# Eighteen attention blocks with their output transposed by DMA, modulations as column tiles, and a third chunk transposed by DMA, in one transformer block on one core

## The chip, the cores and the metric

The kernel runs on one core of a Trainium2 chip. A core has five engines with an instruction queue each: TensorE (PE in the profile) multiplies matrices, VectorE (DVE) and ScalarE (ACT) work element by element, GpSimd (POOL) does small things here, and SyncE (SP) issues transfers. Sixteen DMA engines move data between HBM and the core's SBUF, and within SBUF; transfers are issued from SyncE's queue (q1 in the profile) or ScalarE's (q10). Each engine works through its own queue in order. Matmul results go to eight PSUM banks, from which VectorE or ScalarE evicts them.

The metric is the device time of one execution, in microseconds: the median of several runs.

## The reference

One transformer block for a sequence of 2048 tokens of 448 features, all in bfloat16. A vector `c` gives six modulation vectors; attention has 16 heads of 28 features, and each token sees itself and 7 earlier tokens, at distances 0, 2, ..., 14.

```python
mod = (_silu(c) @ w_mod).reshape(c.shape[0], 6, 1, -1)
sa, ca, ga, sb, cb, gb = (mod[:, 0].copy(), mod[:, 1].copy(), ..., mod[:, 5].copy())
h = _layernorm(x, axis=-1) * (1 + ca) + sa
x = x + ga * _A_ref(h, A_wqkv, A_wo)
h = _layernorm(x, axis=-1) * (1 + cb) + sb
x = x + gb * _B_ref(h, B_w1, B_b1, B_w2, B_b2)
```

`_A_ref` is the attention with its output projection `wo`; `_B_ref` is a second layernorm, `w1` to 1792 features, gelu, and `w2` back to 448.

## The kernel before

**Token order.** All tokens that attend to each other have the same parity, so the kernel keeps even tokens first (1024) and odd tokens after them. In this order a token sees itself and its 7 predecessors: a band. There are 16 token blocks of 128 (`x_all`, line 313), and four chunks of 512 (`CH`).

**Front end** (`front_end`, line 550). For 2 or 4 token blocks: statistics on VectorE (line 446), the reciprocal root on GpSimd (469, 471), normalisation into `zbuf` (477 or 480), then the transposition that puts features on partitions (`hT`). For chunks 0 and 1 that is four TensorE transposes a block (line 577), whose eviction also applies `sa` and `1 + ca` (586, 589). For chunks 2 and 3 (`Z_DMA = (2, 3)`, line 79) it is a DMA transpose from SyncE's queue (line 569), after which VectorE modulates `hT` in place (589). Chunk 0 is done as two halves of 256 tokens. Then come eight projections for q and k (599), each four matmuls of 256 or 512 columns, evicted at 434 or 436.

**Attention** (`attention`, line 664). 17 blocks of 121 queries (`BQ`), each with a window of 128 keys: logits of 16 heads as four row tiles of TensorE (678), four exponentials on ScalarE (689), a product with a mask of 2048 columns on VectorE (696), V (711) and its eviction, the weighted sums with a column of ones for the denominator (721), the division (728, 732). The block's output `on` is transposed by four TensorE transposes (742) and copied from PSUM to `oT` (434 or 436). `oT` feeds the output projection of a token block (`wo_item`, 763), which is added to x (768). Blocks of 121 queries straddle token blocks and the border between even and odd tokens.

**Second half.** For two token blocks at a time (`norm_items`, 770): layernorm, scale and shift (787), second layernorm into `ybuf`, a DMA transpose on SyncE (803). For a chunk (`mlp_items`, 818): the up-projection (295 and 300), gelu on ScalarE (812), the down-projection (853), the last addition (866, 868) and the store (872).

**Modulations.** `sa` and `ca` are made as columns at the start (511). The other four (`mod_item`, 618) are each made with a matrix whose 128 columns all hold silu(c), so that every partition of the result has the vector (623, 448 columns, four matmuls); `ga` is multiplied into `wo_s` (631), `gb` into `w2_s` (648).

**Order.** The instructions of an engine stand in an order that a planner (`Plan.order`, line 108) makes at build time, from costs, due times of the loads (`LANDS`), priorities (`PRI`, `NUDGE`), buffer slots and PSUM banks. `PHASES` says how many attention blocks stand before each chunk's up-projection. The first loads and memsets (355 to 425) come before everything planned; among them the loads of w1 (283, 284) and w2 (425) are SyncE's last before its first transpose. Eight semaphores are used in turn for all transfers, so a transfer is issued only when the one eight places before it has landed.

Of the kernel before, what the change touches and what calls it, by code (L numbers as in the profile page):

```python
# [9 lines left out]
FP32 = mybir.dt.float32  # L10
# [6 lines left out]
KT = 4  # L17
KOFF_N = [0, 128, 256, 320]
ZR_N = 64
# [3 lines left out]
PADF = 16  # L23
BQ, BK = 121, 128
NBK = -(-S // BQ)
WT = PADF + S + PADF
# [5 lines left out]
PHASES = [9, 14, 17, 17]  # L32
# [4 lines left out]
LANDS = [("c", 3.0), ("x0", 5.1), ("wmsa", 6.2), ("wmca", 6.8), ("x2", 8.3), ("wk", 8.6), ("wq", 10.2), ("later", 10.0),  # L37
         ("wv", 11.4), ("x4", 12.4), ("wmod2", 17.4), ("wo", 19.1), ("b2", 19.1), ("x8", 22.0), ("w1", 28.7),
         ("w2", 31.0)]

NIDLE = [8, 3, 3, 4]
PLANS = None

LOOK = 0.000444

PRI = {"ad": -96.0, "agfst": 196.2, "ags2": 257.8, "ags3": 51.1, "ex": -118.3, "ge": -9.0, "h": 492.2,
       "lt": 26.7, "mk": -63.3, "ml": 15.5, "mod": -71.9, "on": -63.1, "ot": -130.2, "pb": -18.2, "po": 77.9,
       "ps": 105.4, "pt": 35.7, "pv": 19.9, "qe": -91.5, "qk": -123.7, "r3": 22.0, "rd": -24.1, "s2": -207.6,
       "s3": 72.9, "ve": -158.2, "w1": -18.3, "w2": -62.8, "wo": -144.0, "wt": 10.8, "x1": 20.5, "y": -37.1,
       "yt": -87.3, "z": 139.3, "z2": 81.0, "zt": -267.4}  # L50

NUDGE = {"ad10": -20.7, "ad6": -81.4, "ad8": 11.5, "ags2_0": 10.6, "ags2_11": -6.6, "ags2_14": -75.9,
       "ags2_2": -100.4, "ags2_5": -6.3, "ags2_8": -10.9, "ags3_11": -15.8, "ags3_14": 104.5, "ags3_3": 36.6,
       "ags3_5": -16.0, "ags3_7": -64.8, "ex11.2": 12.3, "fin9": -40.2, "frs12a": 19.8, "frs8a": 22.6,
       "ge2.10": 13.7, "ge2.8": 76.9, "ge3.12": 31.1, "h12.0": 37.1, "h4.2": 55.2, "h8.2": 78.5, "lt0": 93.2,
       "lt10": 29.5, "lt12": 5.8, "lt13": 52.0, "lt15": -33.2, "lt2": -20.6, "lt4": 58.9, "lt8": -8.9,
       "mk5": 34.4, "mk8": 47.0, "ml10": -42.6, "ml4": 10.8, "on12": -18.4, "on4": 8.5, "ot11": 74.0,
       "ot12": 9.8, "ot16": 53.8, "ot4": 60.9, "ot5": 22.7, "ot6": 65.9, "out13": -24.4, "out14": -59.4,
       "out8": -106.6, "pb_cbe": -184.9, "pb_gb": -36.7, "pb_gbe": -13.6, "po0": 8.9, "po1": -60.3, "po12": 10.8,
       "po15": -157.0, "pt10": 41.4, "pt12": 14.3, "pt5": -52.4, "pt8": -37.2, "pv1": -38.0, "pv13": -62.4,  # L60
       "pv4": 11.4, "pv7": 25.6, "qe12.0": -27.8, "qe12.3": 18.7, "qe12.5": 61.8, "qe2.0": -34.0, "qe2.1": 132.4,
       "qe2.2": 4.0, "qe2.3": 19.6, "qe2.4": 7.9, "qe2.6": 9.4, "qe2.7": -33.6, "qe4.0": 62.7, "qe4.7": -12.7,
       "qe8.0": 5.1, "qe8.1": -64.2, "qe8.7": -80.1, "qk0.1": 133.8, "qk12.0": 113.6, "qk12.6": 61.1,
       "qk4.1": -47.9, "qk4.3": 67.4, "qk4.4": 55.2, "qk4.5": -100.0, "qk4.7": 76.7, "qk8.7": -37.3,
       "r2_0": -89.0, "r2_0a": 57.1, "r2_10": 15.5, "r2_4": -9.3, "r2_6": -40.7, "r2_8": -62.2, "r3_0": 23.2,
       "r3_0a": 24.8, "r3_10a": -7.1, "r3_12": -88.9, "r3_12a": -80.6, "r3_6": 21.3, "r3_6a": -73.9, "r3_8": 9.0,
       "r3_8a": 38.0, "rd12": 24.6, "rd13": 26.1, "rd4": 14.1, "rd6": 54.8, "s2_11": 64.8, "s2_15": -82.0,
       "s2_5": -15.7, "s2_6": 35.8, "s2_8": 10.9, "s3_0": -51.5, "s3_1": 12.8, "s3_10": 26.8, "s3_11": 17.0,
       "s3_12": 28.7, "s3_13": -42.2, "s3_7": 38.2, "s3_9": -24.9, "w1_0.5": 32.1, "w1_1.6": 54.9, "w1_2.0": 6.1,
       "w1_2.2": -19.8, "w1_3.6": 57.3, "w2_11.1": 53.2, "w2_14.2": 103.0, "w2_14.3": 80.6, "w2_14.6": -16.7,  # L70
       "w2_15.2": -35.7, "w2_4.3": -44.4, "w2_5.6": 48.3, "w2_8.2": 135.9, "w2_9.2": 147.8, "w2_9.3": -21.2,
       "w2_9.4": -70.7, "w2_9.5": 107.8, "w2s2": 74.7, "wo0": 8.8, "wo1": 19.3, "wo11": -16.1, "wo8": 34.2,
       "wt_0.5": -16.3, "wt_2.3": -8.1, "wt_2.5": 20.1, "x1_1": 21.7, "x1_10": -25.3, "x1_11": -5.0,
       "x1_5": 27.9, "y11": -18.1, "y5": 40.1, "yt1": 28.5, "yt10": -133.2, "yt11": -10.4, "yt12": -68.4,
       "yt2": 6.1, "z1": 95.3, "z2": 138.5, "z2_10": 23.2, "z2_11": -10.3, "z2_12": -125.8, "z2_13": 16.8,
       "z2_2": 8.2, "z2_4": 21.3, "z2_5": 19.0, "z2_8": 41.6, "z2_9": 13.3, "z4": 6.2, "z8": 12.9, "zt13": -4.0,
       "zt4": 5.5, "zt8": 84.8}
STATS_ACT = 2.0
Z_DMA = (2, 3)
# [160 lines left out]
def kernel(  # L240
# [68 lines left out]
    hT = cst.tile([128, KT, WT], BF16, name="hT")  # L309
    qT = cst.tile([128, 4, WT], BF16, name="qT")  # L310
    kT = cst.tile([128, 4, WT], BF16, name="kT")
# [5 lines left out]
    silu_bc = cst.tile([128, KT, 128], BF16, name="silu_bc")  # L317
# [9 lines left out]
    g2_bc = cst.tile([128, D], BF16, name="g2_bc")  # L327
    sb_bc = cst.tile([128, D], BF16, name="sb_bc")
    gb_bc = cst.tile([128, D], BF16, name="gb_bc")
    gbb2_bc = cst.tile([128, D], FP32, name="gbb2_bc")  # L330
    ident = cst.tile([128, 128], BF16, name="ident")
    mask1 = cst.tile([128, BK], BF16, name="mask1")
    mask_rest = cst.tile([128, H, BK], BF16, name="mask_rest")
# [4 lines left out]
    ybufs = [cst.tile([128, DP], BF16, name=f"ybuf{i}") for i in range(NYB)]  # L338
    NVB = 3
    vbufs = [cst.tile([128, H, DH + 1], BF16, name=f"vbuf{i}") for i in range(NVB)]  # L340

    wmod2 = cst.tile([128, KT, 4 * D], BF16, name="wmod2")
# [3 lines left out]
    silu_bf = cst.tile([128, KT], BF16, name="silu_bf")  # L346
# [9 lines left out]
    wmod = stp.tile([128, KT, 2, DP], BF16, name="wmod")  # L356
    wqk_st = stp.tile([128, KT, 2 * D], BF16, name="wqk_st")
    nc.scalar.dma_start(out=x_all[:, 0:2, :], in_=xv[:, 0, 0:2, :])
    load_ktiles(nc.sync, wmod[:, :, 0, 0:D], w_mod[:, 0:D], 0)
    load_ktiles(nc.scalar, wmod[:, :, 1, 0:D], w_mod[:, D:2 * D], 0)  # L360
    nc.scalar.dma_start(out=x_all[:, 2:4, :], in_=xv[:, 0, 2:4, :])
    load_ktiles(nc.sync, wqk_st[:, :, D:2 * D], A_wqkv[:, D:2 * D], 0)
    load_ktiles(nc.sync, wqk_st[:, :, 0:D], A_wqkv[:, 0:D], 0)
    load_ktiles(nc.sync, Wv, A_wqkv[:, 2 * D:3 * D], 0)
    nc.sync.dma_start(out=x_all[:, 4:8, :], in_=xv[:, 0, 4:8, :])
    load_ktiles(nc.sync, wmod2, w_mod[:, 2 * D:6 * D], 0)
    load_ktiles(nc.sync, wo_s, A_wo, ZR_N)
# [9 lines left out]
    def idle(n, out):  # L377
        for i in range(n):
            nc.tensor.matmul(out, lhsT=idle_in[:, 0:128], rhs=idle_in[:], start=True, stop=True)

    idle(4, psum[7][:])
    c_col = stp.tile([128, KT], FP32, name="c_col")
    nc.vector.memset(c_col[:], 0.0)
    nc.vector.memset(wmod[64:128, KT - 1, :, :], 0.0)
    nc.vector.memset(wmod[:, :, :, D:DP], 0.0)
    nc.vector.memset(Wqk[64:128, KT - 1, :, :], 0.0)
    for zb in zbufs:
        nc.vector.memset(zb[:, D:DP], 0.0)
    nc.vector.memset(Wv[64:128, KT - 1, :], 0.0)
# [21 lines left out]
    def tok_col(b):  # L411
        return PADF + b * 128

# [521 lines left out]
```

## Time and profile before

| what | value |
|---|---|
| time, median of 3 runs | 182.32 us (181.95 to 182.45) |
| the profiled execution | 182.19 us, span 180.5 us |
| granted TensorE clock | 1.00 |
| busy PE / DVE / ACT / POOL | 174.4 / 138.4 / 118.6 / 32.7 us |
| matmuls | 1464 |
| DMA | 14.63 MB, HBM read 9.41 MB |
| q1 (SyncE's queue) | 22334 packets, 13.53 MB |
| q10 (ScalarE's queue) | 1024 packets, 0.86 MB |

The span is the time from the first to the last instruction; the rest of an execution's time lies around it. The profile lists, for each line, engine and shape, how often an instruction ran, how long one took on the mean, and what its engine had waited for. Matmuls overlap, so the mean of one (0.35 us for 448 columns) is its latency and not its price. The chain of waits follows the work back from the last instruction, at each step to what released it; its pieces add up to the span.

### The profile page before, as it was taken

Reading aid. Unit: us, or ns where it says so; the run is one execution under the profiler, and the core shown is the slowest. Engines: PE = TensorE matmul, PEld = TensorE weight load, DVE = VectorE, ACT = ScalarE, POOL = GpSimd, SP = SyncE. Lnnn points to the kernel's source line nnn. Section 1 sums busy time; section 2 is a strip of 40 time slices with the busy share of each in tenths; the row PEclk is TensorE's granted clock in tenths of the full one; section 3 lists DMA queues with packets and bytes.
Section 4 is the critical chain, followed back from the end, with each engine's and each line's share of the span. In section 5 each row is a group of like instructions: output and inputs, shape, how many; then the busy total and the mean of one; then the engine's idle time right before and its main releaser. Section 6 shows DMA issues by size and latency. Waiting matters only on the chain.

```text
span 180.5 us, 3837 instructions
## 1 busy us (share of the span) xinstructions
PE 174.4 (97%) x1464; PEld 88.4 (49%) x1464; DVE 138.4 (77%) x348; ACT 118.6 (66%) x217; POOL 32.7 (18%) x67
## 2 busy tenths in 40 slices
PE   6989999999999999999999999999999999999992
PEld 2457566555555544444655454445643454433451
DVE  5789899799998999997989988688879865020251
ACT  2298996999898946999578475995835810077400
POOL 8413005000106403121403041100013400000000
PEclk9999999999999999999999999999999999999999
DMA  5999995441000530011051012031000025100011
GB/s 166 322 368 315 401 390 162 94 86 29 0 4 0 61 61 0 0 35 32 22 79 35 4 21 63 0 73 41 0 4 25 0 56 120 47 25 0 0 51 51
DMA packets 23376, 14.63 MB, mean 81 GB/s; under 512 B 13693, under 2 KB 22398, under 8 KB 23358
## 3 DMA queue, kind: packets, MB, share of 16 engines
q1 hardware_dynamic: 22334, 13.53, 27.0%
q10 hardware_dynamic: 1024, 0.86, 1.5%
q8 instruction: 11, 0.18, 0.4%
q14 instruction: 7, 0.06, 0.1%
HBM read 9.41 MB, written 1.84 MB: 62 GB/s over the span
## 4 chain that ended last, share of the span: by engine, by line
PE 72%; DVE 12%; DMA 4%; ACT 4%; SPq 2%; issue 2%; ACTq 1%; POOL 1%; DVEq 0%
PE ps L295 21%; PE ps L853 20%; PE ps L599 8%; PE ps L763 6%; PE ps L711 5%; PE ps L300 4%; DVE st L446 4%; DMA hT<-zbuf 3%; PE ps L721 3%; PE ps L678 2%; DVE et L696 2%; PE ps L742 2%; SPq L803 2%; DVE hT L589 2%; DMA yT<-ybuf 1%
## 5 line engine op out<-in xcount | busy, mean ns | idle before, releaser
L812 ACT ACTIVATE hm<-ps,b_col 128x512 bf16<-128x512 f32 x56 | 34.1, 692 | 23.2 <-PE ps L300 23.1
L853 PE MATMUL ps<-w_s,hm 128*128 128x448 bf16 x224 | 47.2, 353 | 0.0
L469 POOL TENSOR_TENSOR rs<-tv,neg_half 128x2 f32<-128x2 f32 (+1 forms) x21 | 20.4, 973 | 108.8 <-DVE ng L465 108.7
L295 PE MATMUL ps<-yT,w_s 128*128 128x512 bf16 x168 | 39.5, 380 | 0.5 <-DMA yT<-ybuf 0.5
L689 ACT ACTIVATE et<-ps 128x512 bf16<-128x512 f32 x68 | 36.1, 613 | 3.3 <-PE ps L678 3.0
L599 PE MATMUL ps<-hT,Wqk 128*128 128x512 bf16 (+1 forms) x160 | 31.3, 337 | 0.9 <-ACT Wqk L436 0.9
L853 PEld LDWEIGHTS <-hm 128*128 128x128 bf16 x224 | 21.0, 98 | 19.3 <-issue 0.9
L295 PEld LDWEIGHTS <-w_s 128*128 128x128 bf16 x168 | 15.5, 98 | 21.9 <-issue 5.3
L866 DVE TENSOR_TENSOR xt<-ps,gbb_bc 128x448 f32<-128x448 f32 x11 | 6.9, 624 | 22.3 <-PE ps L853 22.3
L696 DVE TENSOR_TENSOR et<-et,mask_rest 128x2048 bf16<-128x2048 bf16 x17 | 20.5, 1208 | 0.1
L599 PEld LDWEIGHTS <-Wqk 128*128 128x128 bf16 x160 | 14.6, 97 | 11.4 <-POOL nb L471 1.1
L446 DVE BATCH_NORM_STATS2 st<-x_all 128x6 f32<-128x448 bf16 x32 | 18.5, 613 | 0.1
L711 PE MATMUL ps<-Wv,hT 128*128 128x448 bf16 x68 | 15.7, 353 | 0.0
L763 PE MATMUL ps<-wo_s,oT 128*128 128x448 bf16 x64 | 14.1, 352 | 0.0
L768 DVE TENSOR_TENSOR x_all<-ps,x_all 128x448 bf16<-128x448 f32 x16 | 9.7, 619 | 3.1 <-PE ps L763 3.0
L436 ACT CAST vbuf<-ps 128x448 bf16<-128x448 f32 x14 | 7.6, 546 | 5.0 <-PE ps L711 5.0
L436 ACT CAST qT<-ps 128x512 bf16<-128x512 f32 (+1 forms) x19 | 9.6, 518 | 2.0 <-PE ps L599 1.5
L721 PEld LDWEIGHTS <-et 128*128 128x128 bf16 x272 | 9.0, 96 | 3.8 <-DVE et L696 0.9
L732 DVE TENSOR_TENSOR on<-ps,rden 128x448 bf16<-128x448 f32 x17 | 10.5, 616 | 0.2
L436 ACT CAST kT<-ps 128x512 bf16<-128x512 f32 (+1 forms) x18 | 8.9, 512 | 1.3 <-PE ps L599 1.1
L721 PE MATMUL ps<-vbuf,et 128*128 128x29 bf16 x272 | 9.5, 176 | 0.1
L446 DVE BATCH_NORM_STATS2 st<-z 128x6 f32<-128x448 bf16 x16 | 9.4, 612 | 0.1
(98 smaller groups left out, 188.7 us busy)
## 6 DMA issues: line engine op xcount, KB each, us to landing
w_s<-in_B_w_dram SPq DMA_DIRECT2D x2, 896.0 KB, 11.4
out_dram<-x_all SPq DMA_DIRECT2D x16, 112.0 KB, 1.7
w_s<-in_B_w_dram SPq DMA_DIRECT2D x1, 1568.0 KB, 13.7
wmod<-in_w_mod_dram SPq DMA_DIRECT2D x1, 1344.0 KB, 7.5
x_all<-in_A_x_dram SPq DMA_DIRECT2D x1, 896.0 KB, 10.4
wqk_st<-in_A_wqkv_dram SPq DMA_DIRECT2D x2, 336.0 KB, 5.8
x_all<-in_A_x_dram ACTq DMA_DIRECT2D x2, 224.0 KB, 4.2
x_all<-in_A_x_dram SPq DMA_DIRECT2D x1, 448.0 KB, 5.0
```

The costliest lines, as they stand in the source:

```text
L295: nc.tensor.matmul(o, lhsT=lhs(w, slice(0, 128), kt), rhs=rhs(slice(0, 128), kt), start=(i == 0), stop=False)
L436: nc.scalar.copy(out=out, in_=in_)
L446: nc.vector.bn_stats(out=st[:], in_=src())
L469: nc.gpsimd.tensor_tensor(out=rs[:], in0=T["tv", tile_key][:], in1=neg_half[:, 0:n], op=ALU.pow)
L599: nc.tensor.matmul(pq, lhsT=Wqk[:, kt, m, :], rhs=hT[:, kt, c0:c0 + w], start=(kt == 0), stop=(kt == KT - 1))
L689: nc.scalar.activation(out=et_v[:, r], in_=T["lt", g][r].rearrange("p (ft c) -> p ft c", ft=4), func=ACT.Exp, scale=float(DH) ** -0.5)
L696: nc.vector.tensor_tensor(out=et[:], in0=et[:], in1=mask_rest[:], op=ALU.mult)
L711: nc.tensor.matmul(pv, lhsT=hT[:, kt, k0:k0 + BK], rhs=Wv[:, kt, :], start=(kt == 0), stop=(kt == KT - 1))
L721: nc.tensor.matmul(po[:, h, :], lhsT=T["et", g][:, h, :], rhs=vbufs[g % NVB][:, h, :], start=True, stop=True)
L763: nc.tensor.matmul(pw, lhsT=oT[:, kt, jb * 128:(jb + 1) * 128], rhs=wo_s[:, kt, :], start=(kt == 0), stop=(kt == KT - 1))
L812: nc.scalar.activation(out=T["hm", c][:, ft, 0:w], in_=ps_of(f"p1_{c}.{ft}", w), func=ACT.Gelu_apprx_tanh, bias=b1_col[:, ft:ft + 1])
L853: nc.tensor.matmul(T["p2", b], lhsT=T["hm", c][:, ft, bi * 128:(bi + 1) * 128], rhs=w2_s[:, ft, :], start=(ft == 0 and b not in XPE), stop ...
```

## The change

**Attention blocks.** 18 blocks, nine for each parity: one of 128 queries at the start, then eight of 112. No block crosses the border between parities. The window is 128 keys and ends with the block's last query. Two masks of 128 columns are broadcast over the heads in the product; `mask_rest` and the two memsets on `et` go. `et` and `on` are fixed buffers.

```diff
-BQ, BK = 121, 128
-NBK = -(-S // BQ)
+BLOCKS = [(p * SL + t, n) for p in range(2) for t, n in [(0, BK)] + [(BK + 112 * i, 112) for i in range(8)]]
...
-PHASES = [9, 14, 17, 17]
+PHASES = [9, 16, 18, 18]
...
-Z_DMA = (2, 3)
+Z_DMA = (1, 2, 3)
```

**Output transposed by DMA.** The four TensorE transposes and the copy from PSUM become one DMA transpose on SyncE's queue, from `on` (padded to 512 columns) to `oT`.

```diff
-        def p_fn(e):
-            pt = T["pt", g] = ps_of(f"pt{g}", KT * 64).bitcast(BF16).rearrange("p (kt n) -> p kt n", kt=KT)
-            for kt in range(KT):
-                nc.tensor.transpose(out=pt[:, kt, :], in_=T["on", g][:, KOFF_N[kt]:KOFF_N[kt] + 128],
-                                    identity=ident[:])
...
+        P.add(f"ot{g}", {"SP": 1.25}, needs=[f"on{g}"] + old, uses=[f"on{g}"], lag=1.2,
+              fn=lambda e: nc.sync.dma_start_transpose(out=oT[:, :, c0:c0 + nq], in_=on_of[g][0:nq, :]))
```

**Modulations.** The matrix of silu(c) has 32 columns, and the four vectors are made in one PSUM bank, each in a column tile of 32 (16 matmuls, four column tiles). One eviction adds 1 to `cb`; four rows go to DRAM and come back spread over 128 partitions, both transfers issued from ScalarE's queue. Weights of the modulations are kept as four tiles of 112 rows.

```diff
+    def pb_fn(e):
+        pb = T["pb"] = ps_of("pb", D)
+        for kt in range(KT):
+            for v in range(4):
+                nc.tensor.matmul(pb[32 * v:32 * v + 32, :], lhsT=silu_bc[:, kt, :], rhs=wmod2[:, kt, v * D:(v + 1) * D],
+                                 start=(kt == 0), stop=(kt == KT - 1), tile_position=(0, 32 * v))
...
+    P.add("modw", {"ACT": 0.45}, needs=["pb_e"], lag=2.0,
+          fn=lambda e: nc.scalar.dma_start(out=mod_dram[:], in_=mod_rows[0:128:32, :]))
+    P.add("modr", {"ACT": 0.45}, needs=["modw"], lag=3.0,
+          fn=lambda e: nc.scalar.dma_start(out=mod_bc[:], in_=mod_dram[:].partition_broadcast(128)))
+    P.add("pb_gae", {"DVE": 1.05}, needs=["modr", "wo"], fn=lambda e: nc.vector.tensor_tensor(
+        out=wo_s[:], in0=wo_s[:], in1=mod_bc[:, 0, :].unsqueeze(1).to_broadcast([128, KT, D]), op=ALU.mult))
```

`gb`, `sb` and `1 + cb` are read from `mod_bc` too, where they were copied out of PSUM before.

**Chunk 1.** With `Z_DMA = (1, 2, 3)` the front end of chunk 1 uses DMA transposes as chunks 2 and 3 do. In the order of SyncE's instructions its four transposes stand right after the load of w2, then come two of the attention output, then chunk 2's.

**First loads.** x blocks 0 and 1 come separately on ScalarE's queue, both first modulation matrices in one load, wq and wk in one (three quarters and a rest), and x blocks 2 and 3 on SyncE behind them.

```diff
-    nc.scalar.dma_start(out=x_all[:, 0:2, :], in_=xv[:, 0, 0:2, :])
-    load_ktiles(nc.sync, wmod[:, :, 0, 0:D], w_mod[:, 0:D], 0)
-    load_ktiles(nc.scalar, wmod[:, :, 1, 0:D], w_mod[:, D:2 * D], 0)
-    nc.scalar.dma_start(out=x_all[:, 2:4, :], in_=xv[:, 0, 2:4, :])
-    load_ktiles(nc.sync, wqk_st[:, :, D:2 * D], A_wqkv[:, D:2 * D], 0)
-    load_ktiles(nc.sync, wqk_st[:, :, 0:D], A_wqkv[:, 0:D], 0)
+    for b in range(2):
+        nc.scalar.dma_start(out=x_all[:, b, :], in_=xv[:, 0, b, :])
+    nc.sync.dma_start(out=wmod[:, :, 0:2 * D], in_=w_mod[:, 0:2 * D].rearrange("(kt p) n -> p kt n", p=KM))
+    load_ktiles(nc.sync, wqk_st, A_wqkv[:, 0:2 * D], 0)
+    nc.sync.dma_start(out=x_all[:, 2:4, :], in_=xv[:, 0, 2:4, :])
```

The placement of wq and wk into `Wqk` is done in eight pieces, which may also go to GpSimd. The first transposes use four PSUM banks instead of two. One of the groups of idle matmuls that fill TensorE's first microseconds goes, the others change in size. `LANDS`, `PRI`, `NUDGE` and `LOOK` have new values, so the planner's order is a new one on every engine.

## The prediction

> **What bounds the kernel now.** I read the page's slices first, then busy time by stage, then the chain of waits, then the DMA issues, and the SyncE queue last. The slices (40 of 4.5 us) show TensorE at nine tenths nearly throughout, VectorE close behind until two thirds of the span, and the DMA engines full in slices 2 to 6.
>
> ```profile
> PE   6989999999999999999999999999999999999992
> DVE  5789899799998999997989988688879865020251
> DMA  5999995441000530011051012031000025100011
> ```
>
> By stage (busy us of each engine, granted clock, DMA share, GB/s), both engines are full before 45.6 us, and TensorE alone after it.
>
> ```profile
> 17.00:45.60 28.60, 28.52 (x313) 16.19 (x307) 26.52 (x65) 25.53 (x52) 2.72 (x5) 1.00 0.63 195
> 45.60:66.50 20.90, 20.83 (x214) 11.13 (x214) 20.00 (x53) 18.05 (x35) 5.96 (x8) 1.00 0.18 27
> ```
>
> Busy matmuls overlap, so I take prices from the chain of waits (start, us, what), where each piece is what the next one really had to wait for. From 45.75 on it is an almost unbroken row of matmuls, up to the last addition and store. A group of four transposes of an attention output (L742) costs 0.22 us, a 512-wide projection (L599) 0.86, sixteen weighted sums (L721) 0.40, sixteen logits (L678) 0.34, V (L711) 0.76, one modulation vector (L623) 0.76.
>
> ```profile
> 47.19 0.22 PE ps L742 x4
> ...
> 50.35 0.86 PE ps L599 x4
> 51.22 0.40 PE ps L721 x16
> ...
> 52.48 0.34 PE ps L678 x16
> ...
> 54.65 0.76 PE ps L711 x4
> ...
> 65.72 0.76 PE ps L623 x4
> ...
> 177.33 0.62 DVE x_all L868
> ```
>
> So every microsecond of matmuls taken away is worth up to a microsecond, and every microsecond in which TensorE is left without work costs one.
>
> **What speaks against the change** is in the DMA issues (KB each, us to landing) and in SyncE's own row (start, us).
>
> ```profile
> w_s<-in_B_w_dram SPq DMA_DIRECT2D x1, 1568.0 KB, 13.7
> out_dram<-x_all SPq DMA_DIRECT2D x16, 112.0 KB, 1.7
> x_all<-in_A_x_dram SPq DMA_DIRECT2D x1, 896.0 KB, 10.4
> b_bc<-in_B_b_dram SPq DMA_DIRECT2D x1, 112.0 KB, 9.1
> hT<-zbuf SPq DMA_TRANSPOSE x8, 2.5
> ```
>
> ```profile
> 11.49 0.38 SPq L370 DMA_DIRECT2D x_all<-in_A_x_dram  x1
> ...
> 16.71 0.37 SPq L425 DMA_DIRECT2D w_s<-in_B_w_dram  x1
> 29.42 11.18 SPq L569 DMA_TRANSPOSE hT<-zbuf  x8
> ```
>
> 112 KB take 1.7 us when SyncE's queue is empty (the stores), but 9.1 us for b2, which was issued behind the big modulation load. The queue works off its transfers in the order of issue. The last load, w2, is issued at 16.71 and lands at 16.71 + 13.7 = 30.4. All eight transposes of before were issued from 29.42 on, when that backlog was gone, so their 2.5 us to landing are those of an empty queue.
>
> **The change, part by part.**
>
> *Transposes of the attention output leave TensorE.* 17 groups of 0.22: -3.7 us (up to -5.6 if each also took its mode switch along, as the one of 0.33 at 47.75 did; I take -3.7). Their evictions leave ScalarE (nine, 4.7 us) and VectorE (nine of 0.407, 3.7 us); these engines don't set the end after 45.6, so I count nothing more. In place there are 18 DMA transposes on SyncE, 2.5 us from issue to landing, 1.22 apart (11.18 us hold eight, with waits). Cover: the order puts other matmuls between a weighted sum and the output projection that needs it; where that fails, the bound is 2.5 - 0.6 (0.22 and the 0.41 copy) = 1.9 us for each of 16 output projections.
>
> *18 blocks instead of 17.* One more V, logits and sum: 0.76 + 0.34 + 0.40 = +1.5 us on TensorE. Logits of 112 columns instead of 128 give back at most an eighth of 16 x 0.34, 0.7 us; sixteen such matmuls of 128 columns at 0.34 are 21 ns each, so short that I take a third, -0.2. Masks: 16 x 1.083 (a broadcast product over 1792 elements, the L648 row) + 2 x 1.208 against 17 x 1.208 on VectorE, -0.8, not counted. The two memsets and the 0.69 us of mask_rest go.
>
> *Later modulations as column tiles.* 16 matmuls of 32 columns instead of 16 of 128. If four run side by side, 0.8 us against 4 x 0.76; if they don't, no gain. The nearest row is the logits, which run as four row tiles (21 ns each): I take 0.8, so -2.2 us, and keep 0 as the other bound. The vectors then go through DRAM, two issues on ScalarE's queue. The read of 448 KB is priced by the x load of 448 KB, 5.0 us. The program's order puts its issue on ScalarE behind three evictions of chunk 1's projections; wo_s is scaled on VectorE some 8 us after those become possible, which covers 0.45 + 5.0. Without that cover the first output projection would be up to 3 us late.
>
> *Chunk 1 by DMA.* Its 16 TensorE transposes (1.06 us at 17.99, less overlap) go: -0.9. The four DMA transposes are issued by SyncE after w2, since they follow it in that engine's order and z of chunk 1 is ready only at 17 to 18 us. By the order of the queue they move when x (second half), w1 and w2 are through: 30.4 us. From there the four take between 1.3 us (4 x 128 KB at the 417 GB/s of the loads at 20 to 24 us) and 4.9 us (4 x 1.22, the spacing of before). The last lands at 31.7 to 35.3; I take 33.0, between the ends, as they lie ready in the queue but come in small pieces. The first slice of hT (0.34 us on VectorE) then lets the projections start at 33.3.
>
> When would TensorE want them? From the first projection (10.3 us) the new order has 16 projections of 256 columns (7.0 by 3.06 us for seven), four V (3.0), three logits (1.0), eight transposes (0.57), the modulations (0.8) and two sums (0.8), in all 13.2 us, then chunk 1. With 1.3 us of waits as before (0.9 of them for Wqk) that is 24.8. TensorE stands from 24.8 to 33.3: +8.5 us (from 7 to 10.5). Behind the waiting VectorE instruction stand the first divisions, the third mask and chunk 2's normalisation; on ScalarE an eviction of chunk 1 stands ahead of the last exponential of the third block, which that mask needs. So nothing else can be done early, and the modulation read is late too.
>
> *First loads reordered.* The same bytes; the x blocks 2 and 3 go behind wqk. Before, the first projection at 10.3 was followed by a 0.9 us wait for Wqk. Eight placements now lie on VectorE (five, 0.27), ScalarE (one, 0.56) and GpSimd (two). The latter are not in the trace: between 0.27 and 1.59 each (the longest GpSimd memset). I take 0 for the start, from -0.7 to +1.
>
> *Restart.* After such a pause matmuls may be slow at first: the eight 512-wide ones at 3.50 us took 3.35, 419 ns each, against 215 in the chain. If 3.4 us of work run at half speed that is 1.7; I take 0.9, since VectorE limits just then too. By the Trainium skill ("TensorE: Matmul & The Clock Gate", Part 1) an idle window of 3.4 us halves the clock and 3.4 us of work restore it. By that the term would be the whole 1.7 and the sum 0.8 us higher; no stall of that length stands in the trace of before, and its granted clock reads 1.00 even at the start.
>
> *Sum.* TensorE's work: -3.7 + 1.5 - 0.2 - 2.2 - 0.9 = -5.5, and one idle group of three fewer, before the first projection: not counted. With the pause 8.5 and the restart 0.9: +3.9. As a check, VectorE has some 37 us of work between its wait and the last ybuf of chunk 0 (7 masks 7.4, 8 divisions 4.4, 13 statistics 6.9, 12 slices of hT 4.1, 4 additions 2.3, 4 modulations 2.4, 8 normalisations 3.1, wo_s and two evictions 2.3, small ones 4): 33 + 37 + 2.5 = 72.5 for the first up-projection, which was at 66.44; TensorE's own row gives about 72. The stages after it are shorter by 2.4 us (nine transposes and one output projection fewer, one block of logits more): 72.5 - 66.4 - 2.4 = +3.7 by VectorE, +3.2 by TensorE. I take +3.6. The profiled execution took 182.19 us (span 180.5, 1.7 around it), 0.13 under the median of 182.32; so 185.8.
>
> **Rivals.**
> - *The transposes aren't held by the loads* (they overtake, or the DMA engines serve both). Then the fourth, which waits for the semaphore of the second half of x (11.49 + 10.4 = 21.9), lands at 24.4, just when it's wanted, and the saving stays: 182.2 - 5.5 + 0.3 = 177.0. For it: nothing in the trace shows a transpose behind a load. Against: b2's 9.1 us. This is the one on the other side; it decides if the four land before about 29 us.
> - *Held, but short.* DMA share falls to 0.36 at 28 to 30 us, so most engines are done by 28.7; with a fast drain projections start at 30.3, the pause is 5.5 and the gain pays for it: 182.2.
> - *The output transposes are late as well*: SyncE issues 46 transposes, 56 us in all, in one order with the stores; a third of the 1.9 us at 16 output projections is +10 at worst, +4 if the pause hides part: 189.5. Against: most stand two or more matmul groups ahead of their reader.
>
> **How the numbers follow.** Pause as forecast 0.62 (183 to 188.5), not held 0.16 (176 to 179), held but short 0.09 (180 to 183), late output 0.13 (188.5 to 191). The range from 179 to 190 takes in the first, most of the third and half of the fourth; the forecast's own is 183 to 188.5. A measurement of this kernel can't tell less than about 0.3% (0.5 us) from nothing. Faster: 0.16 + 0.02; same: 0.03; slower: the rest, 0.79.
>
> **What would show it.** In the profile after: the first projection of chunk 1 at 32 to 35 us, with PE idle before it and VectorE's first hT slice ended by the DMA; the group of L742 gone from the chain; the modulation group at about 0.8 us; the first up-projection near 72 us. Wrong, if those slices start at 25 us, or if TensorE finds other work in between.

## The result: 193.9 us, slower by 6%

| | before | after |
|---|---|---|
| median, us | 182.4 | 193.9 (192.4 to 195.5, 4 runs) |
| ratio to before, 95% interval | 1 | 1.061 (1.053 to 1.069) |
| profiled execution, us; its span | 182.2; 180.5 | 195.5; 193.8 |
| TensorE busy, us | 174.4 | 172.9 |
| first up-projection, us from the start | 66.4 | 79.5 |

The forecast was 185.8 with a range up to 190: the direction was right, the size was not. Medians here take in every execution and ratios only the undisturbed ones, so differences between kernels are read from the ratios (0.01 is 1.8 us), and the profile of the kernel after is that of its slowest execution.

The slices of the page after (40 of 4.8 us; busy tenths, granted clock, DMA share) show a hole in TensorE in slices 4 to 8, with VectorE down to 1, the clock below full, and the DMA engines full until slice 7, where before they were full until slice 6.

```profile
PE   7697596099999999899999979999799999999992
DVE  5489461297999999984799779985948775202251
PEclk9889759669999999999999999999999999999998
DMA  5999999829252055211212422120611123100011
```

By stage (length in us, then busy us of PE, PEld, DVE, ACT and POOL, each with its number of instructions, then granted clock, DMA share, GB/s) the stage up to 45.6 us lost ten microseconds of TensorE: 18.63 busy of 28.60, where before 28.52 were.

```profile
17.00:45.60 28.60, 18.63 (x171) 10.80 (x171) 14.92 (x41) 13.37 (x29) 2.69 (x4) 0.76 0.91 217
```

SyncE's row (start, us) shows that the four transposes of chunk 1 directly follow w2 and that issuing them took 12 us; by the list of DMA issues (KB each, us to landing) w2 took 14.4 us, so it landed at 19.74 + 14.4 = 34.1. The load of the later modulations, ahead of it in the queue, took 13.4 us.

```profile
19.74 1.75 SPq L433 DMA_DIRECT2D w_s<-in_B_w_dram  x1
22.44 12.01 SPq L572 DMA_TRANSPOSE hT<-zbuf  x4
```

```profile
wmod<-in_w_mod_dram SPq DMA_DIRECT2D x1, 1568.0 KB, 13.4
w_s<-in_B_w_dram SPq DMA_DIRECT2D x1, 1568.0 KB, 14.4
...
hT<-zbuf SPq DMA_TRANSPOSE x12, 4.1
```

The chain of waits (start, us, what) has the rest: the last transpose lands at 37.5, chunk 1's projections start at 38.44, the first matmuls of them run slowly (ten in 3.82 us, where four take 0.86 before; the granted clock is 0.50 from 38.44 to 42.20), and the read of the modulations, which its issuing engine gets to only then, is not covered any more.

```profile
33.23 4.29 DMA hT<-zbuf
...
38.44 0.61 PE ps L602
...
39.26 3.82 PE ps L602 x10
...
43.11 4.41 DMA mod_bc<-mod_dram
```

TensorE was late ahead of that, too. It waited 1.7 us for ScalarE's part of hT of chunk 0's second half and another 1.7 us, until 22.8, for the 3.5 KB of b1, which stand behind the slow modulation load; after these two waits the granted clock is 0.50 from 22.9 to 28.5, and 32 projection matmuls take 6.35 us, against 3.60 in e16 below. So it came to chunk 1 at 32.1 and stood there for 6.4 us. What it lost before 32.1 is hidden by that pause: chunk 1's normalised blocks were ready at 19.6, and the transposes stood behind w2 whatever TensorE did.

Behind the first up-projection nothing was won either. These are the two stretches from there to the end, first of the kernel before, then of the one after:

```profile
66.44:180.50 114.06, 110.40 (x826) 52.93 (x825) 78.93 (x179) 65.37 (x109) 16.34 (x24) 1.00 0.13 31
```

```profile
79.53:193.80 114.27, 107.67 (x793) 50.29 (x801) 72.94 (x171) 61.88 (x106) 10.68 (x24) 0.99 0.19 41
```

TensorE has 2.7 us less to do (110.40 to 107.67) and the stretch is as long as it was: its idle time grew from 3.7 to 6.6 us.

### The profile page after: what moved, and what is told of

It is laid out like the page before. It is cut to its first block, busy times and chain, and to the rows that moved or that the text cites. A ratio compares the mean times of both kernels' runs of the same rounds, so it can differ in the third digit from the quotient of the medians.

```text
span 193.8 us, 3789 instructions
## 1 busy us (share of the span) xinstructions
PE 172.9 (89%) x1400; PEld 85.7 (44%) x1414; DVE 132.9 (69%) x340; ACT 110.7 (57%) x205; POOL 26.7 (14%) x71
## 4 chain that ended last, share of the span: by engine, by line
PE 61%; DMA 19%; DVE 10%; ACT 3%; SPq 3%; issue 2%; DVEq 0%; ACTq 0%
PE ps L830 21%; PE ps L296 19%; DMA b_row<-in_B_b_dram 6%; PE ps L602 6%; DMA wqk_st<-in_A_wqkv_dram 4%; PE ps L301 4%; PE ps L740 4%; DMA hT<-zbuf 3%; PE ps L702 3%; PE ps L713 2%; DMA mod_bc<-mod_dram 2%; DVE et L695 2%; DMA yT<-ybuf 2%; PE ps L679 2%; DVE st L454 2%
## 5 line engine op out<-in xcount | busy, mean ns | idle before, releaser
L789 ACT ACTIVATE hm<-ps,b_col 128x512 bf16<-128x512 f32 x56 | 33.7, 689 | 22.8 <-PE ps L301 22.7
L830 PE MATMUL ps<-w_s,hm 128*128 128x448 bf16 x224 | 46.2, 353 | 0.0
L296 PE MATMUL ps<-yT,w_s 128*128 128x512 bf16 x160 | 38.9, 380 | 2.5 <-DVE x_all L745 1.3
L688 ACT ACTIVATE et<-ps 128x448 bf16<-128x448 f32 (+1 forms) x72 | 35.1, 564 | 10.1 <-PE ps L679 9.6
L602 PE MATMUL ps<-hT,Wqk 128*128 128x512 bf16 (+1 forms) x155 | 33.8, 373 | 6.9 <-DVE hT L592 6.6
L477 POOL TENSOR_TENSOR rs<-tv,neg_half 128x2 f32<-128x2 f32 (+1 forms) x21 | 15.6, 742 | 129.2 <-DVE ng L473 129.2
L602 PEld LDWEIGHTS <-Wqk 128*128 128x128 bf16 x160 | 16.9, 109 | 20.1 <-DVE hT L592 6.5
L695 DVE TENSOR_TENSOR et<-et,mask 128x1792 bf16<-128x1792 bf16 (+1 forms) x18 | 19.8, 1099 | 1.6 <-ACT et L688 1.6
L444 ACT CAST qT<-ps 128x512 bf16<-128x512 f32 (+1 forms) x17 | 8.9, 524 | 11.1 <-PE ps L602 10.8
L713 PEld LDWEIGHTS <-et 128*128 128x128 bf16 x288 | 9.7, 96 | 3.6 <-DVE et L695 0.6
L764 DVE TENSOR_TENSOR z<-z,mod_bc 128x896 bf16<-128x896 bf16 x16 | 9.8, 615 | 0.3
## 6 DMA issues: line engine op xcount, KB each, us to landing
wmod<-in_w_mod_dram SPq DMA_DIRECT2D x1, 1568.0 KB, 13.4
w_s<-in_B_w_dram SPq DMA_DIRECT2D x1, 1568.0 KB, 14.4
```

The costliest lines, as they stand in the source:

```text
L296: nc.tensor.matmul(o, lhsT=lhs(w, slice(0, 128), kt), rhs=rhs(slice(0, 128), kt), start=(i == 0), stop=False)
L444: nc.scalar.copy(out=out, in_=in_)
L477: nc.gpsimd.tensor_tensor(out=rs[:], in0=T["tv", tile_key][:], in1=neg_half[:, 0:n], op=ALU.pow)
L602: nc.tensor.matmul(pq, lhsT=Wqk[:, kt, m, :], rhs=hT[:, kt, c0:c0 + w], start=(kt == 0), stop=(kt == KT - 1))
L688: nc.scalar.activation(out=et_v[:, r], in_=T["lt", g][r][:, 0:4 * nq].rearrange("p (ft c) -> p ft c", ft=4), func=ACT.Exp, scale=float(DH) ...
L695: nc.vector.tensor_tensor(out=et, in0=et, in1=masks[nq < BK][:, 0:nq].unsqueeze(1).to_broadcast([128, H, nq]), op=ALU.mult)
```

## The experiments

All times against the kernel before on the same chip; e1 to e17 are built on the kernel after, except e8 and e14, which are built on the one before. "Up" is the start of the first up-projection in the profile, "busy" is TensorE's.

| run | median, us | ratio (95%) | up | busy |
|---|---|---|---|---|
| e1 weights behind chunk 1 | 189.9 | 1.028 (1.024 to 1.033) | 76.7 | 171.5 |
| e2 128 rows | 190.7 | 1.046 (1.041 to 1.052) | 74.6 | 171.9 |
| e3 both | 188.0 | 1.029 (1.022 to 1.036) | 74.8 | 171.1 |
| e4 chunk 1 on TensorE, new plan | 196.6 | 1.076 (1.070 to 1.082) | 71.4 | 173.8 |
| e5 weights on ScalarE's queue | 186.9 | 1.024 (1.020 to 1.029) | 71.7 | 169.4 |
| e6 e5, output by TensorE | 193.8 | 1.059 (1.051 to 1.067) | 77.5 | 174.0 |
| e7 chunk 1 on TensorE, plan kept | 183.6 | 1.004 (1.001 to 1.008) | 70.8 | 169.7 |
| e8 before, chunk 1 by DMA | 198.7 | 1.089 (1.085 to 1.093) | 82.9 | 174.8 |
| e9 weights behind the modulations | 191.9 | 1.055 (1.051 to 1.059) | 76.8 | 171.3 |
| e10 e9 with chunk 1 on TensorE | 197.0 | 1.079 (1.072 to 1.086) | 83.2 | 174.6 |
| e11 e7 with 112 rows | 187.7 | 1.030 (1.027 to 1.032) | 73.6 | 171.6 |
| e12 e2 without w1, w2 | 179.9 | 0.987 (0.984 to 0.991) | 65.6 | 167.7 |
| e13 e7 without w1, w2 | 184.9 | 1.012 (1.007 to 1.018) | 69.1 | 169.1 |
| e14 before without w1, w2 | 182.8 | 1.003 (1.002 to 1.004) | 66.5 | 173.3 |
| e15 e7, copies shared | 184.7 | 1.011 (1.005 to 1.017) | 70.4 | 169.4 |
| e16 weights in the queue's gaps | 180.5 | 0.990 (0.987 to 0.992) | 65.0 | 168.2 |
| e17 e16, b1 early | 181.7 | 0.994 (0.991 to 0.997) | 68.1 | 170.0 |

### Which load holds what: e1, e2, e3

e1 issues w1 and w2 behind the transposes of chunk 1:

```diff
-    load_twice(nc.sync, w1_s, B_w1)
-    nc.sync.dma_start(out=w2_s[:], in_=B_w2.rearrange("(ft p) n -> p ft n", p=128))
...
             o["fn"](o["ran"])
+        if o["name"] == "zt7":
+            load_twice(nc.sync, w1_s, B_w1)
+            nc.sync.dma_start(out=w2_s[:], in_=B_w2.rearrange("(ft p) n -> p ft n", p=128))
```

> Edit: the loads of w1 and w2 are issued on SyncE behind chunk 1's four hT transposes instead of ahead of them; nothing else moves, the order of the plan is the same. Theory 'hold' (the transposes stand behind the loads in SyncE's queue): the four land by about 27 us, the first projection of chunk 1 starts at 26 to 29 us instead of 38.4, and of the 10 us that TensorE was idle between 17 and 45.6 us some 6 to 8 come back: 186 to 188 us. Rival 'late stages' (the loss sits in the 18 blocks and the output transposes by DMA, the front is made up for later): projections early, but the time stays at 192 us or more. Rival 'not the queue' (a transpose takes that long by itself while loads run): first projection still past 35 us, 193 to 195 us.

e2 lays w_mod out in rows of 128 again (silu, c and the memsets likewise):

```diff
-    wmod2 = cst.tile([KM, KT, 4 * D], BF16, name="wmod2")
+    wmod2 = cst.tile([128, KT, 4 * D], BF16, name="wmod2")
...
-    nc.sync.dma_start(out=wmod2[:], in_=w_mod[:, 2 * D:6 * D].rearrange("(kt p) n -> p kt n", p=KM))
+    load_ktiles(nc.sync, wmod2, w_mod[:, 2 * D:6 * D], 0)
```

> Edit: w_mod lies in tiles of 128 rows (three of 128 and one of 64 with zeros below) as in the kernel before, not in four tiles of 112 rows; same order of the plan. Theory 'rows' (loads to 112 partitions are slow and push every later load back by 3.7 us): w2 lands at 30 to 31 us instead of 34, the first projection of chunk 1 at 34 to 35 us instead of 38.4, 188.5 to 191 us. Rival 'reordered loads' (the order of the loads, or the two queues, make it slow): w2 still lands past 33 us, and the time stays within 1 us of 193.9. Rival 'late stages': w2 early, but the time stays above 192.

e3 has both edits.

> Edit: both of the two above together. Theories 'hold' and 'rows' share the same idle time of TensorE, so they do not add up: first projection of chunk 1 at 24 to 27 us, TensorE without a pause over 2 us before 45 us, 183 to 186.5 us. 'Late stages': 190 us or more.

e2 answers as "rows" said: 1.046 against 1.061, 2.7 us faster (the two intervals just miss each other, so the size is good to about 2 us), with chunk 1's projections at 34.2 instead of 38.4. In the same four microseconds, in which the changed kernel moves its big modulation load and e2 that load and the next, e2 moved a third more data. First the changed kernel, then e2; the last number is GB/s:

```profile
12.50:16.50 4.00, 4.00 (x42) 3.12 (x43) 3.97 (x15) 3.36 (x9) 0.90 (x2) 1.00 1.05 253
```

```profile
12.50:16.50 4.00, 4.00 (x39) 3.11 (x40) 3.97 (x15) 3.32 (x9) 0.90 (x2) 1.00 1.05 338
```

From 12.8 to 14.0 us, when each of the two moves one transfer only, the rates are 233 and 415 GB/s. All runs agree: 253 to 296 GB/s from 12.5 to 16.5 with 112 rows (the changed kernel, e1, e11), 324 to 341 with 128 (the kernel before and the other fifteen).

e1 and e3 got chunk 1 without a pause, its projections at 29.7 and 25.7. e1's time, 1.028 or 187.5 us, is inside what "hold" said; e3, with both gains, came no further (1.029) and missed its range. The chain of e3 tells why:

```profile
21.46 2.77 DMA hT<-zbuf
...
26.41 13.73 DMA oT<-on
...
41.92 1.00 DVE wo_s L651
...
42.96 1.65 PE ps L743 x4
```

Chunk 1's transposes now take 2.77 us, but the next transposes in the queue, those of the first outputs, stand 13.73 us behind the same 3.2 MB. The read of the modulations, on ScalarE's queue, took 9.9 us beside these loads and landed just as late, at 39.9; TensorE stood 8.0 us for wo, which needs it. The pause had moved, not gone.

### Chunk 1 alone: e4, e7, e8, e11

e4 sets `Z_DMA = (2, 3)` in e2; the planner then makes another order of everything.

> Edit: chunk 1 transposed by TensorE as before, and w_mod in tiles of 128 rows; what is left of the change is the 18 blocks, the output transposed by DMA, the modulations as column tiles spread by DMA and the new order of the loads. The plan is made anew. By the prediction's own terms for these parts (-3.7, +1.5, -0.2, -2.2 against 182.4) it would be 177 to 180 us. 'Late stages' (the output transposes by DMA cost what they save, or more): 182 to 188 us.

It missed the range by the prediction's terms by 17 us and tells little: in its chain TensorE's path goes through the modulations' write and read (4.90 and 5.11 us, from 22.8 to 32.8), and around a late output transpose it is idle for 6.6 of the 20 us from 100 on. The priorities were made for another plan. From here on the order is kept and only the form of an operation changes. e7, on top of e2 (`free_bank` picks a PSUM bank that nothing holds at that place):

```diff
-                P.add(f"zt{b}", {"SP": 1.25}, needs=[f"z{b}"], after=[f"zt{b - 1}"] if i else [], lag=1.2,
-                      fn=lambda e, b=b, zi=zi: nc.sync.dma_start_transpose(
-                          out=hT[:, :, tok_col(b):tok_col(b) + 128], in_=zbufs[zi % NZB][:]))
+                def p_fn(e, b=b, i=i, zi=zi):
+                    if b0 != 4:
+                        nc.sync.dma_start_transpose(out=hT[:, :, tok_col(b):tok_col(b) + 128], in_=zbufs[zi % NZB][:])
+                        return
+                    k = free_bank()
...
+                    for kt in range(KT):
+                        nc.tensor.transpose(out=pt[:, kt * 128:(kt + 1) * 128],
+                                            in_=zbufs[zi % NZB][:, kt * 128:(kt + 1) * 128], identity=ident[:])
+                    copy("ACT", hT[:, :, tok_col(b):tok_col(b) + 128],
+                         pt[:, 0:512].rearrange("p (k n) -> p k n", k=KT))
+                P.add(f"zt{b}", {"SP": 1.25}, needs=[f"z{b}"], after=[f"zt{b - 1}"] if i else [], lag=1.2, fn=p_fn)
```

> Edit: w_mod in tiles of 128 rows, chunk 1 transposed by TensorE into a free PSUM bank with a copy by ScalarE, order of the plan kept as in the changed kernel; w1 and w2 stay ahead on SyncE. Theory 'hold': chunk 1's projections start at 22 to 26 us, but the first output transposes now stand behind w2 and land at 33 to 37 us, so the pause is shorter and later: 184 to 188 us. If chunk 1's transposes alone were held (nothing else late): 180 to 183 us.

e11 is the same on the changed kernel with its 112 rows.

> Edit: the changed kernel with chunk 1 transposed by TensorE (free PSUM bank, copy by ScalarE), plan kept, w_mod in tiles of 112 rows and w1 and w2 ahead on SyncE as they were: chunk 1's transposes alone undone. Theory 'hold' plus 'rows': e7 and the 3 us that the tiles of 112 rows cost, 185.5 to 188 us, against 193.9. If the rows cost only by way of the held transposes of chunk 1: 183 to 185 us.

e7 came out between its two branches and level with the kernel before. e11 came out as "hold" plus "rows" said: with chunk 1 on TensorE the rows of 112 cost 4.6 us (1.030 against 1.004), so they do not cost only by way of chunk 1's transposes.

e8 goes the other way: the kernel before, its order kept, with chunk 1 by DMA.

```diff
+                if b0 == 4:
+                    nc.sync.dma_start_transpose(out=hT[:, :, tok_col(b):tok_col(b) + 128], in_=zbufs[zi % NZB][:])
+                    return
                 if i == 0:
...
-                src = hT[:, kt, c0:c0 + w] if by_dma else T["ptr", b0][kt // 2][:, kt % 2 * 512:kt % 2 * 512 + w]
+                src = hT[:, kt, c0:c0 + w] if by_dma or b0 == 4 else T["ptr", b0][kt // 2][:, kt % 2 * 512:kt % 2 * 512 + w]
```

> Edit, on the kernel before: chunk 1's four blocks transposed by DMA on SyncE in the place where TensorE transposed them, nothing else; order of the plan kept. Theory 'hold': w2 lands at 30.4 us, the projections of chunk 1 start at 33 to 36 us instead of 21.65, TensorE pauses 6 to 10 us, some 0.9 us of transposes are saved: 188 to 192 us. Rival (the hold costs only together with the slow loads or the new plan): under 186 us.

Chunk 1 by DMA costs 7.7 us with 128 rows (e2 against e7) and 5.7 with 112 (the changed kernel against e11), and 16 us in the old order (e8), 7 more than its forecast. There the transposes take as long on SyncE as in the changed kernel, and TensorE waits for ScalarE, in whose order the exponential of the next block stands behind a scaling of chunk 1's hT. These are SyncE's row and the list of TensorE's waits (us, times, longest) of e8:

```profile
18.36 12.65 SPq L575 DMA_TRANSPOSE hT<-zbuf  x4
```

```profile
PE ps L681 <- ACT et L692: 12.9, 1, 12.9
```

So the new order hides part of what the step costs by itself. How much is not settled, since e7 and e11 carry an order made for a late chunk 1 and lose by it; against e16, further down, the step costs 10.3 us. The planner had been told that the transposes come later (they have 1.25 us of issue and 1.2 us of lag there), not that they come at 37 us.

### Another queue: e5, e6, e9, e10

e5 puts the loads of e3 on ScalarE's queue (`nc.scalar` for `nc.sync` in the added lines).

> Edit: w_mod in tiles of 128 rows, and the loads of w1 and w2 issued on ScalarE's queue behind chunk 1's transposes, so that they stand ahead of no transpose on SyncE (in the run with both edits on SyncE the pause only moved: the first output transpose oT<-on stood 13.7 us behind w1 and w2, and wo waited 8 us). Theory 'hold': first projection of chunk 1 at 24 to 27 us, the first output transposes land by 33 us, TensorE without a pause over 2 us between 17 and 66 us, the first up-projection at 66.5 to 69 us, and the 113.5 us behind it as in the other runs: 181 to 184 us. Rival 'bandwidth' (transposes that share the DMA engines with 3.2 MB of loads are slow on any queue): transposes take over 5 us each, first up-projection past 71 us, 185 to 188 us.

e6 is e5 with the output blocks transposed by TensorE, in the manner of e7, with the copy on VectorE.

> Edit: as e5, and the 18 output blocks transposed by TensorE into a free PSUM bank and copied by VectorE in the place where the DMA transpose was issued; the rest of the plan is kept. Theory 'work' (the DMA transposes save TensorE 18 x 0.22 = 4 us and cost some 2 us of waits): 1 to 4 us slower than e5. Rival 'late output' (their waits cost as much as they save): within 1 us of e5 or faster.

e9 (on e2) and e10 (on e7) issue the loads on ScalarE behind `modr` instead of `zt7`.

> Edit: w_mod in tiles of 128 rows, chunk 1 by DMA as in the changed kernel, w1 and w2 on ScalarE's queue behind the modulations' read (in e5 they stood ahead of the modulations' write, which took 11.07 us, and the scaling of wo waited for it until 40.4). Theory 'hold' (all that is wrong with chunk 1 by DMA is what stands ahead of it in a queue): no DMA that something waits for takes over 5 us between 17 and 45 us, TensorE without a pause over 2 us, first up-projection at 66.5 to 69 us and 113.3 us behind it: 181 to 184 us. Rival 'latency' (the DMA route itself, 2.4 us to land and a scaling on VectorE behind four of them, leaves TensorE without work in the front whatever the queue holds): first up-projection at 70 us or later, 185 to 187.5 us as in e5.

> Edit: as e7 (tiles of 128 rows, chunk 1 by TensorE, plan kept), with w1 and w2 on ScalarE's queue behind the modulations' read, so that the first output transposes stand behind no load. Theory 'hold': the first output transposes land 5 us sooner than in e7, first up-projection at 67 to 69.5 us instead of 71.25, 112.2 us behind it: 180.5 to 183 us, 1 to 3 us better than e7. Rival: the pauses of e7 in the front are the plan's own (work put in an order made for a late chunk 1): within 0.7 us of e7, 183 to 184.5 us.

None did what "hold" said. e5 came out where rival "bandwidth" had it; e9 and e10 were slower than either of their theories, e10 by some 13 us. In e5 the victim was the write of 3.5 KB of modulations, which ScalarE issues behind the loads; this is its chain:

```profile
25.55 11.07 DMA mod_dram<-mod_rows
36.64 3.75 DMA mod_bc<-mod_dram
```

In e9 and e10 it was the transposes again, although no load stood ahead of them in their queue: chunk 2's first three took 10.3 to 11.0 us in e9; in e10's chain an output transpose takes 11 us, and its DMA issues have the hT transposes at 9.7 us to landing (the median).

```profile
41.37 11.04 DMA oT<-on
```

```profile
hT<-zbuf SPq DMA_TRANSPOSE x8, 9.7
```

So a second queue doesn't free a transpose of the loads. The Trainium skill ("DMA: Bandwidth & Descriptors", Queues, rings and completion order) has the queues share the DMA engines: each engine takes turns between the queues that have work for it, packet by packet. e10 agrees: the transposes weren't held until the loads had landed, but crept along beside them. The first of chunk 2's, issued at 34.5, landed 10.2 us later at 44.7, and w2, issued at 39.0, only after 13.5 us, at 52.5.

e6 is no clean answer on the output transposes, since chunk 1's pause came back in it (a transpose of hT of 9.84 us in its chain). From the first up-projection to the end, which that pause doesn't touch, it takes 117.5 us against 113.2 of e5: in an order made for it, the output by DMA saves some 4 us there, what "work" counted.

### What the loads cost, and where they don't: e12 to e17

e12, e13 and e14 leave the loads of w1 and w2 out and read the tile of the later modulations in their place, so the MLP computes something else:

```diff
-    w1_s = cst.tile([128, KT, F], BF16, name="w1_s")
+    w1_s = wmod2
+    w2_in = wmod2[:].rearrange("p k (v n) -> p (k v) n", n=D)
...
-    load_twice(nc.sync, w1_s, B_w1)
-    nc.sync.dma_start(out=w2_s[:], in_=B_w2.rearrange("(ft p) n -> p ft n", p=128))
...
-              nc.vector.tensor_tensor(out=w2_s[:, f0:f1, :], in0=w2_s[:, f0:f1, :],
+              nc.vector.tensor_tensor(out=w2_s[:, f0:f1, :], in0=w2_in[:, f0:f1, :],
```

> Edit: as e2 (tiles of 128 rows, chunk 1 by DMA, plan kept), without the loads of w1 and w2: the tile of the later modulations is read in their place, so the MLP's result is another. No transpose stands behind or among 3.2 MB of weights. Theory 'loads' (all of the pause in the front comes from those loads): first projection of chunk 1 at 24 to 27 us, no pause over 2 us, first up-projection at 65 to 68 us, 113.3 us behind it: 180 to 183 us against 190.74. Rival 'latency' (the DMA route leaves TensorE idle by itself): first up-projection at 69 us or later, 184 us or more.

> Edit: as e7 (chunk 1 by TensorE) without the loads of w1 and w2, as in e12. If the savings counted in the prediction (3.7 + 0.2 + 2.2 - 1.5 = 4.6 us of TensorE) are there but were eaten by held output transposes: first up-projection at 66 to 68 us, 177 to 181 us, and 2 us or more faster than the kernel before without these loads. If the savings turn into other waits whatever is loaded: 181.5 to 184 us.

> Edit: the kernel before without the loads of w1 and w2, the later modulations' tile read in their place. Nothing that TensorE waits for stood behind them but chunk 2's first DMA transposes, so 181 to 182.5 us, the same as with them; below 180 would mean that the loads cost the kernel before as well.

e15 is e7 with the four copies of chunk 1 given to VectorE and ScalarE in turns.

> Edit: as e7, with the four copies of chunk 1's transposes out of PSUM shared by VectorE and ScalarE in turns instead of all on ScalarE (in e7 TensorE waited 2.7 us for them). 1 to 2 us faster than e7: 181.5 to 183 us; if the order of the plan sets that stretch, within 0.7 us of e7.

e12 is the answer: without these loads the changed kernel (with 128 rows) is faster than before, by 1.3% against the kernel before and by 1.6% against its twin e14. e14 itself is level with the kernel before (1.003), so these loads cost that kernel nothing. e13 missed: chunk 1 on TensorE gains nothing from the loads' absence, so what is left in e7 is not a hold. e15 missed too: the copies are not it either. Its order was made for a chunk 1 by DMA; which part of that costs the 4 us was not followed further.

e16 brings the loads back, in pieces, where e12's SyncE row has gaps:

```diff
+    piece_after = {"zt7": [(w1_piece, 0), (w1_piece, 1)], "ot1": [(w1_piece, 2)], "zt11": [(w1_piece, 3)],
+                   "zt15": [(w2_piece, 10, 14), (w2_piece, 5, 10), (w2_piece, 0, 5)]}
...
             o["fn"](o["ran"])
+            for piece, *a in piece_after.get(o["name"], ()):
+                piece(*a)
```

> Edit: as e2 (tiles of 128 rows, chunk 1 by DMA, plan kept), with the loads of w1 in four pieces and of w2 in three, on SyncE behind those transposes after which e12 shows its queue empty for some time (after the fourth hT transpose, the second oT, the eighth hT, and all of w2 after the twelfth hT). All loads are there, but no transpose stands behind more than two pieces. Theory 'loads' (the pause is the time that transposes stand behind 3.2 MB): close to e12, 180 to 182 us, faster than the kernel before. Rival (the loads cost their 8 us of DMA time to some transpose wherever they are put, as in e1, e5, e9): 185 us or more.

e17 also moves the load of b1 ahead of `x_all[:, 4:8, :]`.

> Edit: as e16, and the 3.5 KB load of b1 moved ahead of chunk 1's rows of x on SyncE (in e12 TensorE waited 1.5 us for it at 18 to 20 us). If that wait is on the path: 0.8 to 1.5 us faster than e16; if TensorE has to wait for the later modulations' weights there anyway: within 0.5 us of e16.

e16 is 1.0% faster than before (0.8 to 1.3%), and the fastest version that computes the whole block. TensorE gets to chunk 1 at 25.2, close to the 24.8 of the forecast, and goes on at 25.45. Its SyncE row shows each piece behind a group of transposes, its slices TensorE without a hole and at the full clock, and the stage that had lost ten microseconds lacks 2.4:

```profile
17.24 5.23 SPq L583 DMA_TRANSPOSE hT<-zbuf  x4
22.52 1.04 SPq L437 DMA_DIRECT2D w_s<-in_B_w_dram  x2
25.97 3.23 SPq L743 DMA_TRANSPOSE oT<-on  x2
29.26 0.57 SPq L437 DMA_DIRECT2D w_s<-in_B_w_dram  x1
29.92 4.04 SPq L583 DMA_TRANSPOSE hT<-zbuf  x3
...
45.85 1.69 SPq L440 DMA_DIRECT2D w_s<-in_B_w_dram  x3
```

```profile
PE   6989899998999999999998999998999999999992
...
PEclk9999999999999999999999999999999999999999
```

```profile
17.00:45.60 28.60, 26.18 (x308) 14.38 (x297) 26.92 (x70) 24.55 (x52) 4.05 (x6) 1.00 0.88 191
```

The stretch from its first up-projection to the end is 0.9 us shorter than before (113.20 against 114.06), with 2.3 us less for TensorE to do:

```profile
65.00:178.20 113.20, 108.11 (x802) 50.31 (x801) 73.64 (x172) 62.65 (x107) 10.72 (x24) 1.00 0.19 42
```

So it is the loads' place, not their DMA time. e17 missed both branches: it took some 0.8 us more than e16 (0.994 against 0.990). The wait for b1's row, 0.4 us in e16, is gone from its list of waits, but TensorE waits 2.7 us for output transposes instead of 1.7.

## Why the prediction was too low

The runs lead step by step from the kernel before to the kernel after (before, e16, e2, after), so the parts add up by construction; what is measured is the size of each. They are taken from the ratios; the first is good to 0.5 us, the others to 1 to 2 us.

| part | prediction, us | measured, us | from |
|---|---|---|---|
| the change without held transposes | -5.5 | -1.9 | e16 against before |
| chunk 1's transposes held, and the restart | +9.4 | +10.3 | e2 against e16 |
| w_mod in rows of 112 ("first loads") | 0 | +2.7 | after against e2 |
| sum | +3.9 (3.6 taken) | +11.1 | |

- **The hold was right**, in place and cause, and in e2, where the loads run as fast as before, nearly in size: the last transpose lands at 33.3 and chunk 1's projections start at 34.2; the forecast was 33.0 and 33.3. That its sum fits so well is partly luck: the pause is 7.5 us in e2 (TensorE got there at 26.6, not 24.8) instead of 8.5, and the restart 2.4 instead of 0.9. In the changed kernel the pause is 6.4 us, because TensorE was late itself. e16 against e2 shows that the cause is the place of w1 and w2 in the queue. One reading was a little off: before's first transpose was issued at 29.42, 1 us ahead of w2's landing, so the backlog was nearly, not wholly, gone.
- **"First loads reordered. The same bytes", counted at 0, was one wrong step.** The bytes are the same, the rows are not: 112 of 128 partitions, and the loads ran at 253 GB/s where e2 has 338. w2 landed at 34.1 instead of the 30.4 counted on (31.3 in e2), and all that stood behind it moved along. The diff showed the 112 rows; the prediction looked at the order alone.
- **"The stages after it are shorter by 2.4 us", and with it the full -5.5, was the other.** The work did go: TensorE is busy for 168.2 us in e16 against 174.4, 6.2 less, somewhat more than the 5.5 forecast. But only about 2 us of that are time; its idle time grew from 6.1 to 10.0 us. Of these 3.9 us, 2.3 lie between 17 and 45.6 us, in waits of under 0.9 us each (the longest for an output transpose, others of 0.4 for b1's row, for wo and for a masked block), and 1.4 behind the first up-projection, where it waits 0.9 us for an output transpose and 0.9 for a transpose of y. In the changed kernel the waits behind the first up-projection are for an output transpose (1.4 us) and for VectorE's addition ahead of an up-projection (1.3); before had one of 0.5 us there, for a transpose of y. The output transposes were given a bound for such waits and counted at nothing; the rule "every microsecond of matmuls is worth up to one" held as a bound only. That the new order as a whole makes these waits is argued; no run takes the parts of the change one by one.
- **Restart.** Ten matmuls in 3.82 us against 2.15 at 0.86 for four: 1.7 us, not 0.9. The Trainium skill's rule, which the prediction set beside it ("TensorE: Matmul & The Clock Gate", Part 1), gave the 1.7; the changed kernel's trace agrees. In e2 twenty took 6.73 against 4.30, so 2.4, more than that.
- **The modulation column tiles** run side by side, as taken: the group is 0.87 us in e7's chain, not 4 x 0.76. The cover for their read, eight microseconds, was gone, because its issue stood behind the pause: 4.41 us in the chain. In e16, where no pause stands ahead of it, the read takes 5.0 us and TensorE waits 0.4 us for wo, so that cost belongs to the hold.
- **Rivals.** "Not held" didn't happen, but e12 and e16 are that case, made by hand: 180 us, not 177, short by the same missing 3 us. "Late output" is there in the small: TensorE's waits for output transposes add up to 1.4 us in the changed kernel, 1.7 in e16 and 3.3 in e7, not to ten. (Its 189.5 should be 189.8: 185.8 and 4.) None of the rivals held a slower load.

## What to carry to other kernels

Moving work from an engine to a DMA adds a queue to its path: ask what bulk loads stand ahead of it, and what stands behind it when they go; moving the loads only moves the pause until they sit in gaps of the queue. When a diff changes a tile's number of rows, its loads are another operation, even if the bytes are the same. And take a saving at its full size only if the order around it is the same.

## What the runs showed of the hardware

- A load to 112 partitions ran at 253 to 296 GB/s (three runs) in a stretch in which loads to 128 ran at 324 to 341 (the other sixteen). With one transfer under way it was 233 against 415. Why was not tried; the load to 128 rows also comes as two transfers, and no run has that cut alone.
- A transpose in a queue of its own takes up to 11 us beside 3.2 MB of loads on another engine's queue (e10), against 2.4 to 2.5 us in an empty one.
- After a pause of 6.4 or 7.5 us (the changed kernel, e2) the first matmuls cost 1.7 or 2.4 us more, with a granted clock of 0.50; in the changed kernel two waits of 1.7 us with 1.3 us of work between them had the same effect. Runs without such pauses (e12 to e16) have a granted clock of 1.00 over the whole span, the changed kernel 0.953.
